# A new order for the first stretch of an attention and two-MoE kernel, with three PSUM banks for attention's blocks

## The chip, the cores and the metric

The kernel runs on one NeuronCore of a Trainium2 chip. The metric is the device time of one execution in microseconds (us), the median of several. The engines are named as in the profile: PE (TensorE matmul), PEld (TensorE weight load), DVE (VectorE), ACT (ScalarE), POOL (GpSimd) and SP (SyncE, which here only issues DMAs). Each engine has its own queue and takes its instructions in the order in which the kernel writes them.

## The reference, cut to what matters

```python
def _attn_ref(q, k, v, g_norm):                 # 4 batches, 8 heads, 576 tokens, head size 64
    kv = np.einsum('bhsd,bhse->bhde', k, v)
    out = np.einsum('bhsd,bhde->bhse', q, kv)
    rms = np.sqrt(np.mean(out * out, axis=-1, keepdims=True) + 1e-06)
    return (out / rms * g_norm).astype(np.float32)

def _moe_ref(x, w_in, w_out):                   # 2304 tokens, 512 -> 2048 -> 512
    h = x @ w_in
    g = h * (1.0 / (1.0 + np.exp(-h)))
    return (g @ w_out).astype(np.float32)

def _moe2_ref(x, domain_probs, w1, w2):         # 4 experts, 512 -> 1024 -> 512
    p = domain_probs / (domain_probs.sum(-1, keepdims=True) + 1e-09)
    out = np.zeros((N, D), dtype=np.float32)
    for e in range(E):
        h = np.maximum(x @ w1[e], 0.0)
        out += p[:, e:e + 1] * (h @ w2[e])
    return out
```

`reference` runs the three one after the other: attention's output, laid out as 2304 tokens by 512, goes through the first MoE, and its result through the second.

## The kernel before

**Three stages.** Attention gives x, transposed and kept in the SBUF tile `acc`. The first MoE is cut into four groups of 512 hidden units (E1 = 4), the second into eight (E2 = 8). Tokens are cut into three pairs of 768 (t = 0, 1, 2), and each pair into two halves of 384 (HN). Every fp32 operand is split into a high and a low fp32r half: the high one by a copy on ACT (`hi`, line 144), the low one by a subtraction on DVE or POOL (`lo`, line 147). A product is 12 matmuls of 128x384. In all but the first group, seven products stand in for eight (operands `b11`, `b21`, `t1` to `t4`, `b22` of x, where the `t` are differences made by `xsum`, line 317); the first group (`plain`, line 372) multiplies eight plain products per pair.

**Steps.** The steps are numbered n = -12 to 23: three pairs times four groups with n below 0, then three pairs times eight. `start[n]` gives a step its place in slots; a slot is as long as one product. `events` (line 612) and `first_events` (line 519) put every operation at a slot, the list is sorted, and that sorted list is each engine's order. n = -12 and n = -11 are the first group's pairs 0 and 1, n = -1 is the last step of the first MoE, n = 0 the first of the second, n = 8 and n = 16 begin the second MoE's pairs 1 and 2.

**The first stretch** is not in `events`. `PROGRAM` (line 36) writes its order out by hand, one word for each operation, and `attention_moe_kernel` issues the words one by one. What the words mean, with the engine:

- `lkv:b:c`, `lq:g`, `lwd:c:i` (SP): loads of a chunk of k and v (512 KB, the fifth chunk of a batch 256 KB), of 384 tokens of q (768 KB), of a chunk of the first MoE's raw weights (512 KB).
- `xp:t:name` (SP): store of a split operand of x to DRAM (768 KB); it waits until both halves are there.
- `kv:b:c` (PE): eight matmul records that add a chunk to k-transposed-v of batch b. `bda`, `bdv` (ACT, DVE): copy it out of PSUM.
- `om:i` (PE): attention's block i of 128 tokens (18 blocks). Then a chain for each block: `sq` (ACT, squares), `red` (DVE, sums), `rms` (POOL, power -0.5), `sc` (DVE, scales, frees the PSUM bank), `tr` (PE, transposes), `xc` (ACT, copies to `acc`).
- `cv1`, `cv2` (ACT), `cv3`, `cv4` (DVE), `cv5` (POOL): turn a chunk of raw weights into fp32. `wh`, `wl`, `vh`, `vl`: the two halves of the first group's first and second weights.
- `xh`, `xl`, `xt`: high half, low half and difference of x's operands. A trailing `:p` puts a low half on POOL, otherwise it is on DVE.
- `f:b:d`, `f1:b:d` (PE): product d of block b of `plain` for pairs 0 and 1. `si`, `hh`, `hl`: SiLU and the two halves of the hidden tile. `ready` closes attention's pools and opens those of the hidden tiles and second weights.

**Banks and buffers.** PSUM has eight banks. Four belong to `ps1`, as two buffers of two banks which `bank` (line 157) hands out by i % 2; `plain` takes number b + 1. Attention has `ps_o` (2 banks, for `om`), `ps_t` (1) and `ps_kv` (1). k and v of batches 1 to 3 have seven buffers, q has three, raw weights two; batch 0's chunks lie in x's own buffers. Buffers are freed when the last use stands in the order.

## Time and profile before

| | us |
|---|---|
| three runs, median (lowest to highest) | 1211.57 (1209.32 to 1212.93) |
| the profiled execution, its own time | 1213.71 |
| its span, from first to last instruction | 1211.9 |
| PE busy in the span | 1170.5 |
| DVE, ACT, POOL busy | 814.6, 482.5, 296.0 |

The time of the profiled execution is 1.8 us above its span and 2.1 us above the median. PE's records include time in which a matmul is in the pipeline, so its busy share says where PE is free, not how fast it runs. The mean granted clock of the span is 0.992 of full speed.

### The profile page before, as it was taken

To read this page: it belongs to the slowest core of one execution; us is meant where nothing else is said; L and a number is where in the kernel's file an instruction comes from. 1 tells how busy PE (TensorE), PEld (TensorE's weight loads), DVE (VectorE), ACT (ScalarE), POOL (GpSimd) and SP (SyncE) were. 2 spreads that over 40 slices of the span, in tenths; PEclk is the share of its full clock that TensorE was granted. 3 is DMA by queue.
4 is the path that set the end of the run, shared out by engine and by line. 5 is a ranking of instruction groups with operands and counts; after the bars stand their busy time and mean duration, and the time that the engine had idled before them with its cause. 6 is when DMAs were issued, how large, how long until landed. Compare 5 with 4: busy or idle time off the path is not lost.

```text
span 1211.9 us, 17576 instructions
## 1 busy us (share of the span) xinstructions
PE 1170.5 (97%) x6789; PEld 1158.8 (96%) x6789; DVE 814.6 (67%) x940; ACT 482.5 (40%) x693; POOL 296.0 (24%) x191
## 2 busy tenths in 40 slices
PE   6779999999999999999999999999999999999998
PEld 6679999999999989999999999999999899999997
DVE  2468775546544365767777876777788876666676
ACT  2457575435443242543444433333333242333222
POOL 2573331111210033323322311111113211111112
PEclk8999999999999998999999999999999999999999
DMA  9734798657655616797889687989898677778763
GB/s 315 261 108 187 255 346 307 234 194 246 236 171 175 215 70 222 276 325 277 295 304 329 236 283 261 352 294 339 304 350 295 239 239 259 274 261 267 260 215 122
DMA packets 105895, 309.00 MB, mean 255 GB/s; under 512 B 11532, under 2 KB 42708, under 8 KB 105812
## 3 DMA queue, kind: packets, MB, share of 16 engines
q1 hardware_dynamic: 103796, 304.69, 72.0%
q10 hardware_dynamic: 2016, 3.18, 0.7%
q8 instruction: 54, 0.88, 0.3%
q14 instruction: 29, 0.24, 0.1%
HBM read 227.84 MB, written 79.99 MB: 254 GB/s over the span
## 4 chain that ended last, share of the span: by engine, by line
PE 71%; DVE 10%; ACT 4%; issue 3%; DMA 2%; POOL 1%; SPq 1%; DVEq 0%; ACTq 0%; POOLq 0%
PE ps_o L481 21%; PE ps_x L356 19%; PE ps_z L356 15%; PE ps_ox L356 9%; PE ps_oz L356 7%; DVE hid L148 2%; DVE acc L321 2%; ACT hid L145 1%; DVE f L433 1%; ACT x L145 1%; DVE w L148 1%; DVE acc L456 1%; DVE f L399 1%; DVE x L148 1%; DMA w_dram<-w 1%
## 5 line engine op out<-in xcount | busy, mean ns | idle before, releaser
L481 PE MATMUL ps_o<-hid,w 128*128 128x384 f32 x1920 | 359.7, 337 | 6.3 <-ACT hid L145 3.5
L481 PEld LDWEIGHTS ps_o<-hid,w 128*128 128x128 f32 x1920 | 335.8, 189 | 9.6 <-ACT hid L145 4.1
L356 PE MATMUL ps_x<-x,w 128*128 128x384 f32 x1584 | 298.0, 336 | 1.9 <-ACT x L145 1.9
L356 PEld LDWEIGHTS ps_x<-x,w 128*128 128x128 f32 x1584 | 278.3, 189 | 2.2 <-ACT x L145 2.2
L356 PE MATMUL ps_z<-x,w 128*128 128x384 f32 x1188 | 222.7, 335 | 0.1
L356 PEld LDWEIGHTS ps_z<-x,w 128*128 128x128 f32 x1188 | 207.5, 188 | 0.7 <-ACT f L409 0.4
L145 ACT ACTIVATE hid<-f 128x768 fp32r<-128x768 f32 x128 | 107.8, 844 | 235.3 <-DVE f L433 230.2
L148 DVE TENSOR_TENSOR hid<-f,hid 128x768 fp32r<-128x768 f32 x111 | 122.6, 1106 | 75.1 <-ACT hid L145 73.9
L356 PE MATMUL ps_ox<-hid,w 128*128 128x384 f32 x768 | 144.9, 337 | 0.2 <-issue 0.2
L356 PEld LDWEIGHTS ps_ox<-hid,w 128*128 128x128 f32 x768 | 134.1, 188 | 0.5 <-issue 0.5
L148 POOL TENSOR_TENSOR hid<-t,hid 128x768 fp32r<-128x768 f32 x32 | 60.9, 1905 | 243.2 <-ACT hid L145 237.6
L356 PE MATMUL ps_oz<-hid,w 128*128 128x384 f32 x576 | 108.3, 336 | 2.0 <-DVE acc L456 1.9
L356 PEld LDWEIGHTS ps_oz<-hid,w 128*128 128x128 f32 x576 | 100.4, 188 | 3.2 <-DVE acc L456 2.5
L145 ACT ACTIVATE hid<-t 128x768 fp32r<-128x768 f32 x64 | 53.9, 843 | 122.1 <-DVE t L438 122.1
L148 POOL TENSOR_TENSOR w<-raw,w 128x512 fp32r<-128x512 f32 x41 | 60.5, 1481 | 163.1 <-ACT w L145 120.1
L456 DVE TENSOR_TENSOR acc<-ps_o,acc 128x768 f32<-128x768 f32 x64 | 60.9, 951 | 42.2 <-PE ps_o L481 41.9
L203 POOL TENSOR_TENSOR full<-full,wd_raw 128x512 int32<-128x512 int32 x32 | 47.2, 1474 | 143.1 <-DVE full L197 118.5
L399 DVE TENSOR_TENSOR f<-ps_z,f 128x768 f32<-128x768 f32 x66 | 62.8, 951 | 25.2 <-PE ps_z L356 25.2
L456 DVE TENSOR_TENSOR acc<-ps_ox,acc 128x768 f32<-128x768 f32 x57 | 54.2, 950 | 36.6 <-PE ps_ox L356 36.6
L433 DVE SCALAR_TENSOR_TENSOR f<-f,pb 128x768 f32<-128x768 f32 x72 | 72.5, 1007 | 2.1
L394 ACT ACTIVATE f<-ps_x 128x768 f32<-128x768 f32 x66 | 52.9, 802 | 50.5 <-PE ps_x L356 50.5
L148 POOL TENSOR_TENSOR hid<-f,hid 128x768 fp32r<-128x768 f32 x17 | 31.7, 1867 | 150.3 <-ACT hid L145 142.7
(79 smaller groups left out, 1113.5 us busy)
## 6 DMA issues: line engine op xcount, KB each, us to landing
w<-w_dram SPq DMA_DIRECT2D x224, 512.0 KB, 4.9
w_dram<-w SPq DMA_DIRECT2D x112, 512.0 KB, 4.1
x<-x_dram SPq DMA_DIRECT2D x63, 768.0 KB, 5.0
raw<-in_w SPq DMA_DIRECT2D x192, 128.0 KB, 3.7
wd_raw<-in_wd SPq DMA_DIRECT2D x32, 512.0 KB, 4.7
...
```

The source lines that it names most:

```text
L145: self.nc.scalar.activation(t[:, 0], f, AF.Copy)
L148: (eng or self.nc.vector).tensor_tensor(t[:, 1], f, t[:, 0].bitcast(F32), op=ALU.subtract)
L203: self.nc.gpsimd.tensor_tensor(f, f, self.words(c, i, 0, I32), op=ALU.add)
L321: self.nc.vector.tensor_tensor(o, a, b, op=ALU.subtract)
L356: self.nc.tensor.matmul(p[:, f, :HN], w[0][:, a, c : c + 128], x[:, b, kp, :], start=self.FRESH[k] and a == b == kp == 0, stop=b == kp == ...
L394: self.nc.scalar.activation(t, self.of_ps(n, c), AF.Copy)
L399: self.nc.vector.tensor_tensor(t, self.of_ps(n, c), t, op=ALU.add)
L433: self.nc.vector.scalar_tensor_tensor(f, src, 0.0, self.probs(n, int(name[2]) - 1), op0=ALU.max, op1=ALU.mult)
L456: self.nc.vector.tensor_tensor(a, self.of_ps(n, k), a, op=ALU.add)
L481: self.nc.tensor.matmul(self.ps[n, b][:, e, :HN], w[:, u, c : c + 128], h[:, v, kp, :], start=self.count[key] == 1, stop=self.count[key] = ...
```

## The change

It has five parts. (1) `PROGRAM` has the same operations in another order; eight low halves change their engine (`wl:2`, `xl:1:b11`, `vl:21`, `xl:0:t1`, `xl:0:t2`, `xl:0:t4` go from DVE to POOL, `wl:1` and `xl:0:b22` from POOL to DVE). All loads but `lwd:1:1` now stand ahead of the first store `xp`. (2) `ps_o` has three banks; `ps_kv` is gone, and `kv` uses a buffer of `ps1` with number b. (3) A split operand of x that is stored is dropped only after both its store and its last product (`done_x`), since either can now come first. (4) In `first_events` block 2 of pair 1's `plain` comes before the second product of pair 0, with its SiLU; `xget` of two operands of step n = -9 comes 1.4 and 1.7 slots earlier; at n = -1 the hidden block c12 gets SiLU and both halves sooner. (5) In `events` the second MoE's first weights (n = 0) are loaded 3.5 slots and converted, and stored, 2.7 slots earlier, and `xsum` of t1 for pairs 1 and 2 comes 4.7 slots earlier.

```diff
@@ -34,26 +34,26 @@
 
 
 PROGRAM = """
-lkv:0:0 lkv:0:1 lkv:0:2 kv:0:0 lkv:0:3 kv:0:1 lkv:0:4 kv:0:2 lq:0 kv:0:3 lwd:0:0 kv:0:4 bda:0 bdv:0 lwd:1:0
-om:0 om:1 lkv:1:0 sq:0 red:0 sq:1 rms:0 lkv:1:1 cv1:0:0 red:1 cv2:0:0 sc:0 rms:1 cv1:1:0 sc:1 lkv:1:2 tr:0
-kv:1:0 xc:0 cv3:0:0 cv2:1:0 tr:1 lkv:1:3 cv4:0:0 xc:1 kv:1:1 cv3:1:0 om:2 lkv:1:4 cv5:0:0 lq:1 kv:1:2 sq:2
-red:2 wh:0 kv:1:3 cv4:1:0 rms:2 sc:2 lq:2 cv5:1:0 kv:1:4 bda:1 tr:2 bdv:1 xc:2 wl:0 wh:1 om:3 lkv:2:0 xh:0:b11
-wl:1:p om:4 sq:3 lkv:2:1 xh:0:b21 red:3 xl:0:b11 rms:3 sq:4 lkv:2:2 sc:3 xl:0:b21:p xp:0:b11 kv:2:0 red:4 tr:3
-lkv:2:3 xc:3 kv:2:1 rms:4 xp:0:b21 sc:4 om:5 lkv:2:4 lwd:2:0 kv:2:2 sq:5 red:5 tr:4 kv:2:3 xc:4 lwd:3:0 rms:5
-sc:5 kv:2:4 tr:5 lq:3 bda:2 om:6 xc:5 bdv:2 om:7 sq:6 red:6 f:0:0 lkv:3:0 sq:7 rms:6 cv1:2:0 red:7 cv2:2:0
-sc:6 rms:7 lkv:3:1 cv1:3:0 sc:7 tr:6 om:8 xc:6 cv3:2:0 lkv:3:2 sq:8 kv:3:0 cv4:2:0 cv2:3:0 red:8 tr:7 cv5:2:0
-lkv:3:3 xc:7 kv:3:1 rms:8 cv3:3:0 wh:2 om:9 lkv:3:4 xh:0:b12 sc:8 lq:4 kv:3:2 sq:9 cv4:3:0 tr:8 red:9 kv:3:3
-cv5:3:0 xc:8 xh:0:b22 lq:5 kv:3:4 rms:9 wl:2 om:10 bda:3 wh:3 xl:0:b22:p bdv:3 f:0:1 sc:9 sq:10 lwd:0:1 red:10
-xp:0:b22 xl:0:b12 rms:10 tr:9 lwd:1:1 si:c11 sc:10 wl:3:p om:11 xc:9 om:12 sq:11 div wx tr:10 sq:12 f:1:0
-red:11 xc:10 red:12 cv1:0:1 rms:11 sc:11 rms:12 cv2:0:1 sc:12 tr:11 cv1:1:1 om:13 cv3:0:1 xc:11 cv2:1:1
-cv4:0:1 tr:12 cv3:1:1 sq:13 om:14 xc:12 red:13 cv5:0:1 f:1:1 sq:14 red:14 rms:13 lwd:2:1 rms:14 sc:13 si:c21
-sc:14 tr:13 om:15 cv4:1:1 xc:13 xt:0:t1 tr:14 sq:15 om:16 xc:14 red:15 cv5:1:1 turn sq:16 f:2:0 keepp red:16
-rms:15 lwd:3:1 xh:1:b11 sc:15 rms:16 xh:1:b21 sc:16 tr:15 om:17 xl:1:b21:p xc:15 tr:16 sq:17 f:2:1 xc:16
-red:17 xp:1:b21 cv1:2:1 xl:1:b11 rms:17 cv2:2:1 sc:17 xp:1:b11 f:3:0 si:c12 cv3:2:1 cv1:3:1 cv4:2:1 cv2:3:1
-tr:17 cv3:3:1 f:3:1 xc:17 cv5:2:1 xh:0:t1 ready hh:c11 cv4:3:1 f1:0:0 hh:c21 hl:c11 si:c22 hl:c21 hh:c12
-f1:0:1 cv5:3:1 hh:c22 xh:1:b12 hl:c12 f1:1:0 si1:c11 hl:c22 xh:1:b22 xl:1:b12 vh:11 f1:1:1 xl:1:b22 vh:12
-vh:21 vl:11 xp:1:b22 vh:22 vl:12:p si1:c21 vl:21 vl:22:p xl:0:t1 vx xt:0:t2 xp:0:t1 xh:0:t2 xt:0:t3 xl:0:t2
-xh:0:t3 xl:0:t3 xp:0:t2 xt:0:t4 xh:0:t4 xp:0:t3 xl:0:t4 xp:0:t4
+lwd:0:0 lkv:0:2 lkv:0:0 cv1:0:0 cv2:0:0 cv3:0:0 lkv:0:1 cv4:0:0 lkv:0:3 cv5:0:0 kv:0:0 wh:0 lq:0 kv:0:1 wl:0
+kv:0:2 lkv:0:4 kv:0:3 lkv:1:1 lkv:1:4 kv:0:4 lkv:1:0 bda:0 bdv:0 om:0 lkv:1:3 sq:0 om:1 lkv:1:2 red:0 om:2
+sq:1 rms:0 red:1 kv:1:0 sq:2 lwd:1:0 red:2 kv:1:1 rms:1 sc:0 lq:1 tr:0 kv:1:2 xc:0 rms:2 sc:1 kv:1:3 cv1:1:0
+lq:2 tr:1 cv2:1:0 cv3:1:0 kv:1:4 xc:1 sc:2 bda:1 om:3 cv4:1:0 lkv:3:1 bdv:1 cv5:1:0 tr:2 sq:3 om:4 xc:2 red:3
+lwd:3:0 xh:0:b11 rms:3 xh:0:b21 om:5 lkv:2:4 xl:0:b11 lkv:2:0 sq:4 sc:3 xl:0:b21:p wh:1 red:4 om:6 sq:5
+lkv:2:1 cv1:3:0 tr:3 red:5 rms:4 f:0:0 sq:6 cv3:3:0 lwd:2:0 cv2:3:0 red:6 rms:5 xc:3 cv4:3:0 kv:2:0 lkv:3:0
+sc:4 kv:2:1 rms:6 sc:5 lkv:2:2 wl:1 om:7 cv1:2:0 cv5:3:0 tr:4 sq:7 lkv:2:3 om:8 sc:6 cv2:2:0 red:7 f:0:1 xc:4
+cv3:2:0 lwd:0:1 rms:7 sq:8 wh:3 red:8 tr:6 cv4:2:0 lkv:3:2 si:c11 rms:8 kv:2:2 sc:7 xc:6 kv:3:0 lq:3 cv5:2:0
+cv1:0:1 tr:7 kv:2:3 sc:8 xc:7 wl:3:p wh:2 kv:3:1 lkv:3:3 cv2:0:1 kv:2:4 wl:2:p kv:3:2 bda:2 lkv:3:4 bdv:2 tr:8
+lq:4 cv3:0:1 wx om:9 xc:8 cv4:0:1 tr:5 sq:9 kv:3:3 cv5:0:1 xc:5 red:9 lwd:2:1 om:10 xh:0:b22 rms:9 kv:3:4
+xh:0:b12 xl:0:b22 lwd:3:1 om:11 bda:3 xl:0:b12 sq:10 f:1:0 lq:5 sq:11 sc:9 cv1:2:1 bdv:3 red:10 cv2:2:1 tr:9
+red:11 rms:10 cv1:3:1 om:12 cv3:2:1 xc:9 f:1:1 sq:12 div rms:11 cv2:3:1 xp:0:b22 xp:0:b11 xp:0:b21 sc:10 turn
+xh:1:b11 f:2:0 sc:11 keepp xl:1:b11:p red:12 si:c21 xh:1:b21 tr:10 om:13 rms:12 cv4:2:1 xc:10 xp:1:b11 cv3:3:1
+xt:0:t1 tr:11 sq:13 om:14 xc:11 red:13 cv5:2:1 f:2:1 xh:0:t1 sc:12 sq:14 rms:13 cv4:3:1 lwd:1:1 red:14 om:15
+si:c12 xt:0:t2 rms:14 tr:12 sq:15 sc:13 f:3:0 xc:12 red:15 cv5:3:1 xh:0:t2 sc:14 cv1:1:1 tr:14 rms:15 xt:0:t3
+cv2:1:1 om:16 cv3:1:1 xc:14 f:3:1 sq:16 sc:15 xl:1:b21:p xh:0:t3 red:16 tr:15 xh:1:b22 rms:16 cv4:1:1 om:17
+xp:1:b21 xc:15 xl:1:b22 f1:0:0 sq:17 xl:0:t3 xp:1:b22 xh:1:b12 sc:16 cv5:1:1 si:c22 xp:0:t3 tr:13 red:17
+f1:0:1 xc:13 xl:1:b12 rms:17 xt:0:t4 tr:16 sc:17 xl:0:t1:p f1:1:0 xc:16 xl:0:t2:p xp:0:t1 tr:17 f1:1:1 xc:17
+ready vh:21 hh:c11 vl:21:p xp:0:t2 hh:c21 hl:c11 hh:c12 hl:c21 si1:c11 hh:c22 hl:c12 si1:c21 hl:c22 vh:11
+vh:12 vl:11 vh:22 vl:12:p xh:0:t4 vl:22:p xl:0:t4:p vx xp:0:t4
 """
 
 
@@ -88,7 +88,7 @@
         for n in range(self.steps):
             self.start[n + 1] = self.start[n] + (self.LONG if n <= E2 else self.SHORT)
         self.stacks = {}
-        self.begun, self.count = set(), {}
+        self.begun, self.used, self.count = set(), set(), {}
         self.x, self.w1, self.wf, self.w2, self.raw, self.s, self.h, self.f, self.t, self.ps, self.pb = (
             {} for _ in range(11)
         )
@@ -338,8 +338,14 @@
     def xput(self, n, name):
         t = self.x[n, name].bitcast(F32).rearrange("p a b c -> p (a b c)")
         self.nc.sync.dma_start(out=self.x_dram[self.pair(n) * 7 + self.B.index(name)], in_=t)
-        if name[0] == "t":
+        self.done_x(n, name)
+
+    def done_x(self, n, name):
+
+        if name[0] == "t" or name == "b12" or (n, name) in self.used:
             del self.x[n, name]
+        else:
+            self.used.add((n, name))
 
     def xget(self, n, k):
         t = self.new_x(n, self.B[k], k).bitcast(F32).rearrange("p a b c -> p (a b c)")
@@ -385,7 +391,7 @@
                         )
         if i == d == 1:
             for k in range(2):
-                del self.x[n, f"b{k + 1}{j + 1}"]
+                self.done_x(n, f"b{k + 1}{j + 1}")
         if self.pair(n) == NP - 1 and j == 1:
             del self.wf[0, 2 * i + d]
 
@@ -531,10 +537,11 @@
                             put(b0 + 0.1 + b, self.hhi, n, name)
                             put(b0 + 0.2 + b, self.hlo, n, name)
                             continue
+                    ahead = t == 1 and b == 2
                     for d in range(2):
-                        put(at + 1 + 2 * d, self.plain, n, b, d)
+                        put(b0 - 0.4 + 0.1 * d if ahead else at + 1 + 2 * d, self.plain, n, b, d)
                     late = 2 if t == 1 else 0
-                    for slot, f in ((4.05, self.silu), (4.95 + late, self.hhi), (5.4 + late, self.hlo)):
+                    for slot, f in ((-0.1 if ahead else 4.05, self.silu), (4.95 + late, self.hhi), (5.4 + late, self.hlo)):
                         put(at + slot, f, n, name)
             elif e > 0:
                 for k in range(7):
@@ -546,9 +553,10 @@
                     put(b0 + slot, f, n, c, name)
                 put(b0 + 12.2, self.ps.pop, (n, "z"))
                 for slot, name in ((4.2, "c11"), (10.2, "c22"), (12.2, "c12"), (14.0, "c21")):
-                    put(b0 + slot + 0.02, self.silu, n, name)
-                    put(b0 + slot + 0.5, self.hhi, n, name)
-                    put(b0 + slot + 1, self.hlo, n, name)
+                    soon = n == -1 and name == "c12"
+                    put(b0 + slot + (-0.09 if soon else 0.02), self.silu, n, name)
+                    put(b0 + slot + (-0.08 if soon else 0.5), self.hhi, n, name)
+                    put(b0 + slot + (0.1 if soon else 1), self.hlo, n, name)
             blocks = self.blocks(n)
             for b, (i, j) in enumerate(blocks):
                 for d in range(2):
@@ -605,7 +613,7 @@
                 for k in range(7):
                     at = 2 * k - 12.4
                     if n == NP - F1:
-                        at = (-6.8, -6.7, -0.6, -4, -3.5, -0.5, 0.5)[k]
+                        at = (-6.8, -6.7, -0.6, -5.4, -5.2, -0.5, 0.5)[k]
                     put(b0 + at, self.xget, n, k)
         put(-24, self.swap)
 
@@ -629,14 +637,14 @@
                     of = {"t1": b0 - 11.5, "t2": b0 - 7.5, "t3": b0 - 6.5, "t4": b0 - 4.5}
                 else:
                     at = [last + k for k in (2.2, 4, 8.2, 6.3)] + [b0 + k for k in (6.2, 3, 8.2)]
-                    of = {"t1": last + 5.9, "t2": last + 7.7, "t3": b0 + 5.5, "t4": b0 + 7.3}
+                    of = {"t1": last + 1.2, "t2": last + 7.7, "t3": b0 + 5.5, "t4": b0 + 7.3}
                 for k, name in enumerate(self.B):
                     put(at[k], self.xhi, n, name)
                     put(at[k] + 0.01, self.xlo, n, name, pool if k in (1, 3, 5) and t == 0 or k in (0, 1, 5) and t else None)
                 for name, s in of.items():
                     put(s, self.xsum, t, name)
 
-            lead = self.LEAD + (2.5, -2)[n] if n < 2 else self.LEAD
+            lead = self.LEAD + (5.2, -2)[n] if n < 2 else self.LEAD
             for k in range(7):
                 i = b0 + 1 + 2 * k
                 put(i, self.first, n, k)
@@ -654,7 +662,7 @@
                 put(i - lead + 2, self.put_away, n, 1, k)
             if make:
                 for k, (i, j) in enumerate(((1, 0), (1, 1), (0, 0), (0, 1))):
-                    put(b0 - (self.LEAD + 5 if n else 20) + 0.5 * k, self.load1, n, i, j)
+                    put(b0 - (self.LEAD + 5 if n else 23.5) + 0.5 * k, self.load1, n, i, j)
                 for k, name in ((4, "a11"), (4, "a21"), (5, "a12"), (6, "a22"), (3, "s1"), (4, "s3"), (5, "s2"), (5, "s4")):
                     put(b0 + 1.01 + 2 * k - lead, self.raw.pop, (n, 1, name))
             put(b0 + 2.1, self.keep, n, "x", "c11")
@@ -798,9 +806,8 @@
     o_p = on(early, "o", 2)
     small_p = on(early, "small", 4)
     bd_p = on(early, "bd", 1)
-    ps_o = on(psum, "ps_o", 2, space=PSUM)
+    ps_o = on(psum, "ps_o", 3, space=PSUM)
     ps_t = on(psum, "ps_t", 1, space=PSUM)
-    ps_kv = on(psum, "ps_kv", 1, space=PSUM)
     squares = [bd_p.tile([128, H, D + 1], F32, tag=f"sq{i}", name=f"sq{i}") for i in range(2)]
     half = bd_p.tile([128, H], F32, tag="half", name="half")
     kvbd = [bd_p.tile([128, KC, 128], F32, tag=f"kvbd{i}", name=f"kvbd{i}") for i in range(B)]
@@ -827,7 +834,7 @@
 
     def kvm(b, c):
         if c == 0:
-            kv_ps[b] = ps_kv.tile([128, KC, 128], F32, tag="kv", name="p_kv")
+            kv_ps[b] = net.bank(net.ps1, b, "kv")[:, 0].rearrange("p (k n) -> p k n", k=KC)
         n, r = min(128, S - c * 128), kv_raw.pop((b, c))
         for hp in range(KC):
             cols = slice(hp * 128, hp * 128 + 128)
```

## Rows read from the trace of the kernel before

**Rows 1.** Page, part 1: busy us of the engines, share of the span, instructions.

```profile
PE 1170.5 (97%) x6789; PEld 1158.8 (96%) x6789; DVE 814.6 (67%) x940; ACT 482.5 (40%) x693; POOL 296.0 (24%) x191
```

**Rows 2.** Stretches: length, busy us (x instructions) of PE, PEld, DVE, ACT, POOL, clock, DMA, GB/s.

```profile
0.00:50.00 50.00, 31.77 (x206) 29.58 (x207) 14.91 (x24) 14.81 (x25) 19.15 (x24) 0.91 0.83 277
50.00:100.00 50.00, 42.49 (x295) 40.09 (x293) 33.61 (x52) 31.23 (x51) 33.64 (x21) 0.95 0.51 172
...
0.00:10.00 10.00, 3.12 (x13) 2.83 (x14) 0.15 (x1) 1.49 (x2) 2.72 (x14) 1.00 0.78 240
10.00:20.00 10.00, 7.55 (x45) 6.86 (x44) 1.82 (x3) 2.39 (x5) 0.82 (x1) 1.00 1.04 374
```

**Rows 3.** Waits of PE: who for whom, us in total, times, the longest.

```profile
PE p_t L881 <- DVE o L875: 13.7, 8, 3.4
```

**Rows 4.** Groups by line, PE, 0 to 107.7 us: busy, mean ns, idle before.

```profile
L382 PE MATMUL ps_h<-x,w 128*128 128x384 f32 x144 | 26.8, 340 | 0.0
L834 PE MATMUL p_kv<-kv_raw 128*128 128x128 f32 (+1 forms) x160 | 26.3, 322 | 9.2 <-DMA kv_raw<-in_kv 9.2
L855 PE MATMUL p_o<-kvbd,q_raw 128*128 128x128 f32 (+1 forms) x160 | 21.6, 300 | 2.7 <-DVE o L875 1.7 <-DVE kvbd L842 1.0
L881 PE MATMUL p_t<-ident,o 128*128 128x128 f32 x72 | 13.1, 312 | 13.8 <-DVE o L875 13.7
```

**Rows 5.** Timeline of PE, first stretch: start, us, instruction, [idle before <-releaser].

```profile
16.50 2.05 PE L855 MATMUL p_o<-kvbd,q_raw 128*128 128x128 f32 x16 [0.99 <-DVE kvbd L842]
...
39.63 0.63 PE L881 MATMUL p_t<-ident,o 128*128 128x128 f32 x4 [3.42 <-DVE o L875]
40.09 1.06 PE L834 MATMUL p_kv<-kv_raw 128*128 128x128 f32 x8
...
107.76 2.18 PE L481 MATMUL ps_o<-hid,w 128*128 128x384 f32 x11 [0.67 <-DVE w L148]
```

**Rows 6.** Chain of work that ended last, one full product: start, us, what.

```profile
178.02 2.08 PE ps_o L481 x12
```

**Rows 7.** Groups by line, 0 to 180 us: attention's chain, and POOL's low halves of x.

```profile
L870 POOL TENSOR_TENSOR rinv<-ssq,half 128x8 f32<-128x8 f32 x18 | 32.3, 1802 | 31.5 <-DVE ssq L866 31.5
...
L875 DVE TENSOR_TENSOR o<-p_o,rinv 128x512 f32<-128x512 f32 x18 | 12.5, 692 | 19.9 <-POOL rinv L870 19.9
...
L866 DVE TENSOR_REDUCE ssq<-sq 128x8 f32<-128x520 f32 x18 | 12.3, 690 | 11.9 <-ACT sq L862 11.8
...
L862 ACT ACTIVATE sq<-p_o 128x512 f32<-128x512 f32 x18 | 10.7, 595 | 11.4 <-PE p_o L855 10.6 <-DVE ssq L866 0.7
...
L148 POOL TENSOR_TENSOR x<-acc,x 128x768 fp32r<-128x768 f32 x4 | 7.5, 1874 | 12.1 <-ACT x L145 12.1
```

**Rows 8.** Timeline of SP's queue, first stretch (merged issues of one line).

```profile
19.56 5.23 SPq L818 DMA_DIRECT2D kv_raw<-in_kv  x3
37.32 0.33 SPq L340 DMA_DIRECT2D x_dram<-x  x1
```

**Rows 9.** Timeline of PE, DVE and ACT where the second MoE begins.

```profile
449.63 0.67 DVE L280 TENSOR_TENSOR s<-raw,raw 128x512 f32<-128x512 f32 x1
...
452.69 0.83 ACT L145 ACTIVATE hid<-f 128x768 fp32r<-128x768 f32 x1
...
453.57 1.06 PE L481 MATMUL ps_o<-hid,w 128*128 128x384 f32 x4 [2.66 <-ACT hid L145]
...
455.56 2.93 PE L481 MATMUL ps_o<-hid,w 128*128 128x384 f32 x8 [0.92 <-DVE hid L148]
...
458.28 3.56 PE L356 MATMUL ps_x<-x,w 128*128 128x384 f32 x12
```

**Rows 10.** Timeline of POOL, DVE and PE before the second MoE's third pair.

```profile
935.28 1.89 POOL L148 TENSOR_TENSOR hid<-t,hid 128x768 fp32r<-128x768 f32 x1 [2.57 <-ACT hid L145]
935.38 2.61 DVE L321 TENSOR_TENSOR acc<-acc 128x768 f32<-128x768 f32 x1
...
940.78 2.36 PE L356 MATMUL ps_oz<-hid,w 128*128 128x384 f32 x12 [1.62 <-DVE acc L456]
```

## Prediction

> **What bounds the kernel now.** I read the page first: PE is busy 97% of the span, every other engine 67% or less [rows 1], so time can only come from PE's idle time and from PE's slow clock. I then cut the span into stretches of 50 us. From 100 us on nearly all are full; the first two have 31.8 and 42.5 us of PE work and a mean clock of 0.91 and 0.95 [rows 2]. The list of PE's waits has one large item: 13.7 us, in eight waits, in which a transpose waits for the scaled block from DVE [rows 3]; the groups by line add 9.2 us of waiting for k and v [rows 4]. I looked at two later places because the change touches them: the first step of the second MoE [rows 9] and the step before its third pair [rows 10].
>
> To size the first stretch I count its work at the full clock. Two starts in the timeline, 39.63 and 40.09, make a block's transposes 0.46 us; the kv chunk after it is shown as 1.06 us, but the next instruction group starts 0.89 us later, since the ends of matmuls overlap [rows 5] (a chunk of kv and a block of om both have eight records). A full product takes 2.08 us [rows 6]. Before the first product with second weights PE does 20 chunks, 18 blocks, 18 transposes and 12 plain products [rows 4]: 17.8 + 16.0 + 8.3 + 25.0 = 67.1 us. That product really starts at 107.8 us [rows 5], so 40.7 us are lost. The first block starts at 16.5 us [rows 5] with 4.5 us of work done: 12.0 lost at the start, 28.7 later. Of these, 13.7 + 1.7 us are PE waiting for the scaled block [rows 4], some 7.0 us are slow clock (50 x 0.09 + 50 x 0.05 [rows 2]), some 2 us a late third wait for k and v.
>
> **The change part by part. First stretch, the chain.** Between a block's `om` and its `tr` stand four steps: 0.60, 0.69, 1.80 and 0.69 us [rows 7], 3.8 us, and with the handovers about 4.2 (an estimate). I added up the PE work that the two orders put between `om:i` and `tr:i`. Before, it is less than 4.2 us in 14 of 18 blocks (0.9 us for block 0, 1.8 for block 3), 16.8 us short in all, close to the 15.4 us that PE waits; that agreement is why I trust the count. In the new order only blocks 0 and 3 are short (3.6 and 3.1 us), 1.7 us in all. Three banks make this order possible, since three or more blocks are then under way. If POOL has one low half (1.87 us [rows 7]) ahead of each power, the chain is 5.9 us, five blocks are short and 6.7 us remain. I take 5, near the upper end, since POOL also has eight `cv5` and more low halves there: gain 15.4 - 5 = **10.4 us**, from 8.7 to 13.7.
>
> **The start.** `om:0` needs the last chunk of batch 0. Ahead of it and with it now come 3.67 MB (a raw weight chunk and q are in front) instead of 2.36 MB. 240 GB/s over the first 10 us and 374 after it [rows 2] put these at 13.4 and 9.8 us: **3.6 us later**, from 1.5 (part of that time PE was behind the data) to 5.
>
> **Loads and stores.** SP takes its list in order. Before, it issued k and v until 24.8 us and then nothing until 37.3 us, where a store of x was released [rows 8]; the loads behind that store stood still. Now all of these loads stand ahead of the stores, and SP can stop only where a buffer is still read; the tightest is `lwd:3:1`, ten words behind the `cv5:0:1` that frees it. I put the late wait for k and v at nothing: gain **2 us**, from 0 to 2.3. The stores pay for it. `xp:0:b22`, `b11` and `b21` now stand just ahead of `xh:1:b11` and `xh:1:b21`, which write the same buffers, so ACT waits for 2.36 MB to be read: 6.3 us at 374 GB/s and the landing. Behind ACT's wait are `keepp`, `si:c21` and `xc:10`, for which PE's `tr:11` waits; between the store's last operand and `tr:11` PE has three blocks, three products and two transposes, 9.8 us. So 0 to 3 us, I take 1. `kv:3:0` now waits for `si:c11`, which frees its bank: 1.35 us of PE work between, against a SiLU behind one square and one weight half on ACT: 0 to 1, I take 0.4. At `ready` the second weights (`vh`, `vl`) are now the last words, but two plain products (4.2 us) are put ahead of the first product that needs them: 0 to 3, I take 1, where 0.67 us stand now [rows 5]. New waits: **2.4 us**, from 0 to 7.
>
> **Clock.** With long idle gaps the clock falls, and 7.0 us went that way. One fall, at the start, I leave in place; gain **2.5 us**, from 0 to 4. The first stretch: 10.4 + 2 + 2.5 - 3.6 - 2.4 = 8.9 us gained.
>
> **DVE against POOL.** Six low halves go to POOL and two come back. An operation of DVE that started 0.10 us behind one of POOL took 2.61 us, and ended 0.82 us after POOL's, which took 1.89 us [rows 10]; it looks as if it stood still for the other's remaining 1.79 us and then ran. The Trainium skill, "SBUF — State Buffer", section "Who interferes with whom", says that an instruction of DVE with two inputs in SBUF and one of POOL that reads SBUF share a port pair held for the whole instruction, so that the second one waits; these rows agree. By that rule each further meeting costs DVE up to one POOL operation, and the rule speaks against the change. By the rows the price of a meeting is up to 1.79 us on DVE; four more meetings are 7.2 us of DVE, on an engine that is idle half of the first 100 us [rows 2]. I count none of it on PE beyond the 5 us above; it sets a rival.
>
> **First step of the second MoE.** PE waits 2.66 us for the high half of c12 and 0.92 us for its low half; then a third of a product takes 2.93 us over eight matmuls and the next product 3.56 us [rows 9] instead of 1.39 and 2.08 [rows 6], some 2.8 us of slow clock after allowing for the drawn-out ends: 6.4 us. The change takes one 0.67 us weight sum from in front of c12's addition on DVE (s1 and s2 move ahead of that stretch, s4 enters it, s3 stays) and one conversion of x, 0.83 us like c12's own, from in front of c12's high half on ACT [rows 9]. The 2.66 us become 1.2, the low half still waits 0.9. A single wait of 1.62 us elsewhere left the product behind it at 2.36 us [rows 10], so I expect full clock: gain 1.5 + 2.8 = **4.3 us**, from 0.7 to 6.4. The earlier loads, conversions and stores of these weights pass `load_p` and `load2` on SP; they have 11 slots of lead as before, so I cost them at nothing. If a weight half came late, one product would wait some 2 us.
>
> **Third pair.** The difference that took 2.61 us on DVE moves ten us earlier, to a place with idle time; the sum for which PE waits 1.62 us [rows 10] comes earlier by more than that: gain **1.6 us**, 0 to 1.9. For the second pair the same move has no wait to remove. The two earlier `xget` have no wait of PE behind them either: nothing.
>
> **Sum.** 8.9 + 4.3 + 1.6 = 14.8. I give back 0.8 because PE then meets the next weight conversions sooner: 14.0. The profiled execution took 1213.7 us; less 14.0 is 1199.7. It lies 2.1 us above the median of the runs, so the median becomes 1211.6 - 14.0 = 1197.6: **1198 us**.
>
> **The rivals.** A measurement of this kernel tells 0.3%, 3.6 us, from no change. *POOL carries the chain*: the powers queue behind conversions and low halves, 8 us of waits remain and the slow clock stays, so the first stretch gives about 1 us; with the rest, 6 gained: 1206. For it: POOL is busy 33.6 of the second 50 us already [rows 2]; against: it is the same work over nearly the same time. *The waits only move*: ACT stands behind the stores the full 3 us, the handover costs 3, the clock still falls, and c12 gains only its lower end: nothing in the first stretch, 2 elsewhere: 1210, no change. *More than forecast*: all ends good, 13.7 + 2.3 + 4 - 1.5 in the first stretch and 8.3 elsewhere: 1186. *Slower*: POOL's low halves and `cv5` hold DVE's sums and scales up, in the stretch from 20 to 100 us. If twelve meetings of 1.79 us [rows 10] come on the chain, 21.5 us are added and 7.5 remain lost: 1219; from ten meetings on it is slower by more than 3.6 us. Against it: all but four of these operations stand there already, and the chain's count fitted without it. The Trainium skill's rule on the shared port pair (same page and section) would make this the outcome if each further meeting fell on the chain; the trace shows the meetings but not that they reach PE.
>
> **How the numbers follow.** Forecast (9 to 20 us gained) 0.50; more 0.11; POOL carries the chain 0.22; the waits only move 0.10; slower 0.07. So faster 0.83, same 0.10, slower 0.07. The range of 1186 to 1209 takes in all ends but the last two cases, about 0.15 left out.
>
> **What would show it.** Right: waits of `p_t` for DVE fall from 13.7 to some 5 us; SP shows no gap from 25 to 37 us; the first block starts near 20 us and the first product with second weights, now behind two more products, before 102 us; the 2.66 us wait halves and the products behind it are at 2.1 to 2.4 us; the 1.62 us wait is gone. Wrong: a first block after 24 us, ACT waiting for the stores, a new long wait of PE after 100 us, or `rms` waiting in POOL's queue with `p_t` as before.

## The result and the profile after

| | before | after |
|---|---|---|
| median of 4 runs each (us) | 1212.15 | 1192.10 |
| lowest to highest (us) | 1209.32 to 1212.93 | 1191.13 to 1193.36 |
| profiled execution (us) | 1213.7 | 1192.07 |
| its span (us) | 1211.9 | 1190.3 |

One run of the kernel before was added to the three shown ahead. The ratio is 0.9839, with a 95% interval of 0.982 to 0.9858. The median falls by 20.0 us where 14.0 were forecast. 1192 lies inside the range of 1186 to 1209, but at the far end of the case that I called the forecast (9 to 20 us gained).

The first fence holds rows of the changed kernel that answer to [rows 1] and [rows 2]: the engines' busy time on the page, then two stretches of 50 us (length, then busy us of PE, PEld, DVE, ACT and POOL, granted clock, DMA share, GB/s).

```profile
PE 1162.4 (98%) x6789; PEld 1153.9 (97%) x6789; DVE 803.6 (68%) x936; ACT 482.2 (41%) x693; POOL 303.1 (25%) x195
...
0.00:50.00 50.00, 37.34 (x265) 35.50 (x266) 20.85 (x36) 22.13 (x37) 26.60 (x30) 0.93 0.96 311
50.00:100.00 50.00, 45.87 (x316) 43.79 (x316) 34.54 (x51) 35.30 (x55) 35.40 (x22) 1.00 0.53 202
```

PE is busy for 9 us more in these 100 us, and the clock of the second stretch rose from 0.95 to 1.00. The next view is the list of PE's waits in the changed kernel (who for whom, us in total, times, the longest); it answers to [rows 3].

```profile
PE ps_kv L841 <- DMA kv_raw<-in_kv: 10.0, 2, 8.0
PE ps_o L487 <- ACT hid L145: 3.1, 2, 2.6
PE ps_h L388 <- ACT f L415: 2.2, 1, 2.2
PE ps_x L362 <- ACT x L145: 1.9, 1, 1.9
PE p_t L888 <- ACT p_t L907: 1.4, 1, 1.4
PE p_o L862 <- DVE o L882: 1.3, 1, 1.3
...
PE p_t L888 <- DVE o L882: 0.4, 1, 0.4
```

The 13.7 us for DVE's scaled block [rows 3] are 0.4 now; with the 1.3 us in front of one `om`, 1.7 us are left of the 15.4. Of the 10.0 us for k and v, 8.0 are the start before any data is there. Two waits are new: `ps_h` for ACT (2.2) and `p_t` for ACT (1.4). The timeline of PE in the changed kernel shows where they sit, and the two landmarks of [rows 5] (start, us, instruction, [idle before <-releaser]). The single row behind it is from the kernel before.

```profile
19.43 4.73 PE L862 MATMUL p_o<-kvbd,q_raw 128*128 128x128 f32 x24 [0.98 <-issue]
...
66.63 0.66 PE L888 MATMUL p_t<-ident,o 128*128 128x128 f32 x4 [1.41 <-ACT p_t L907]
...
92.72 4.45 PE L388 MATMUL ps_h<-x,w 128*128 128x384 f32 x24 [2.22 <-ACT f L415]
97.01 6.41 PE L487 MATMUL ps_o<-hid,w 128*128 128x384 f32 x36
...
437.13 2.65 PE L487 MATMUL ps_o<-hid,w 128*128 128x384 f32 x12 [2.58 <-ACT hid L145]
...
947.73 3.81 PE L362 MATMUL ps_x<-x,w 128*128 128x384 f32 x12 [1.86 <-ACT x L145]
```

```profile
106.76 0.34 PE L481 MATMUL ps_o<-hid,w 128*128 128x384 f32 x1
```

The first product with second weights starts at 97.0 us. In the kernel before its first matmul stands at 106.8, ahead of the row of [rows 5], and the other eleven go on at 107.8; the end of the product is 10.7 us earlier in the changed kernel. Two more plain products (4.2 us) are done by then: 14.9 us ahead. Following the same products through both timelines gives the whole balance: 14.9 us at 97 us; 16.4 in front of the second MoE's first step, by small differences on the way that I did not follow; 20.0 behind that step; 20.5 in front of the third pair and 22.4 behind the wait of 1.62 us [rows 10], which is gone; 23.0 at 947.7; and 21.6 behind the product there and at the end, because that product takes 3.81 us where before, behind the same wait of 1.86 us, it took 2.36. That is the whole difference of the two profiled executions, 1213.7 - 1192.1 = 21.6. It is one execution of each kernel, and the last section shows that three pieces of it came out otherwise in other kernels with the same waits.

### The profile page after: what moved, and what is told of

The parts are those of the page before. It is cut to its first block, busy times and chain, and to the rows that moved or that the text cites. A ratio compares the mean times of both kernels' runs of the same rounds, so it can differ in the third digit from the quotient of the medians.

```text
span 1190.3 us, 17575 instructions
## 1 busy us (share of the span) xinstructions
PE 1162.4 (98%) x6789; PEld 1153.9 (97%) x6789; DVE 803.6 (68%) x936; ACT 482.2 (41%) x693; POOL 303.1 (25%) x195
## 3 DMA queue, kind: packets, MB, share of 16 engines
q10 hardware_dynamic: 2016, 3.18, 0.8%
## 4 chain that ended last, share of the span: by engine, by line
PE 80%; DVE 7%; DMA 5%; ACT 3%; issue 3%; POOL 2%; SPq 0%; POOLq 0%; DVEq 0%; ACTq 0%
PE ps_o L487 24%; PE ps_x L362 21%; PE ps_z L362 16%; PE ps_ox L362 9%; PE ps_oz L362 7%; DMA x_dram<-x 1%; ACT hid L145 1%; DVE f L439 1%; DVE acc L321 1%; DVE hid L148 1%; PE ps_kv L841 1%; ACT x L145 1%; DMA x<-x_dram 1%; DMA kv_raw<-in_kv 1%; PE p_o L862 1%
## 5 line engine op out<-in xcount | busy, mean ns | idle before, releaser
L145 ACT ACTIVATE hid<-f 128x768 fp32r<-128x768 f32 x128 | 107.8, 844 | 232.8 <-DVE f L439 227.7
L148 DVE TENSOR_TENSOR hid<-f,hid 128x768 fp32r<-128x768 f32 x111 | 119.9, 1082 | 79.4 <-ACT hid L145 78.3
```

Of the source, the lines that this page charges most:

```text
L145: self.nc.scalar.activation(t[:, 0], f, AF.Copy)
L148: (eng or self.nc.vector).tensor_tensor(t[:, 1], f, t[:, 0].bitcast(F32), op=ALU.subtract)
```

## The experiments

Four questions: what the two halves of the change are worth; what in the first stretch does it (cover, banks, stores, start); why the wait at 437 us did not halve; and whether the waits that are left can be taken away. Ratios are always to runs of the kernel before on the same chip.

**The later edits alone, and the order alone.** The first kernel is the kernel before with the change's edits of `events` and `first_events` (and the release of x operands that they need); PROGRAM and the PSUM banks stand as before. The second is the changed kernel with those edits undone.

```diff
# the later edits (added to before; taken back from after)
-put(at + 1 + 2 * d, self.plain, n, b, d)
+put(b0 - 0.4 + 0.1 * d if ahead else at + 1 + 2 * d, self.plain, n, b, d)
...
-"t1": last + 5.9,
+"t1": last + 1.2,
...
-lead = self.LEAD + (2.5, -2)[n] if n < 2 else self.LEAD
+lead = self.LEAD + (5.2, -2)[n] if n < 2 else self.LEAD
...
```

> The kernel before with only the later edits (block 2 of pair 1 ahead, c12 sooner, second experts' first weights earlier, xsum of t1 and xget earlier); the first stretch keeps its old order, its two banks and its stores among the loads. Theory (the first stretch carries the gain): only the later edits' part is left, 3.6 us at the second MoE's first step, 1.9 us before its third pair and up to 1 us at the handover, so some 1206 us (1204 to 1208). Rival (the later edits carry most of it): below 1200 us.

Measured: 1207.9 us, 0.9961 (0.9943 to 0.998), at the upper end of what was expected. The wait in front of c12 is 2.61 us in this kernel too.

> The changed kernel with the later edits undone: new order of the first stretch, three banks, stores behind the loads, and the old slots everywhere else. Theory (the first stretch carries the gain): some 1197 us (1195 to 1200), with the 2.7 and 0.9 us waits and the slow clock back at the second MoE's first step and the 1.6 us wait back before its third pair. Rival: above 1203 us.

Measured: 1199.9 us, 0.99 (0.9886 to 0.9915). The order with its three banks is worth 11.6 us and the later edits 3.7, together 15.3; the whole change gives 20. The gap of 4 to 5 us is hardly clear of the spread: the interval of the first ratio alone reaches from 2.4 to 6.9 us gained. PE's waits in the kernel with the order alone:

```profile
PE ps_o L487 <- ACT w L145: 4.2, 1, 4.2
PE ps_o L487 <- ACT hid L145: 3.7, 3, 2.7
```

With the new order PE gets to the second weights before they are converted (4.2 us). The two plain products put ahead fill about half of that hole (2.2 us are left in the changed kernel), and that gain of 2 us shows in neither half alone. The profiled executions miss 4.3 us (21.6 against 3.5 and 13.8): 1.4 are missing behind the handover to the second weights, and 1.6 more behind the second MoE's first step, where the later edits alone left two slow products (3.29 and 3.22 us) and the whole change one nearly full one (2.65). So a part of the gap is the speed of single products behind a wait, told of in the last section.

**The cover.** The count of PE work between `om` and `tr` says that 14 blocks are short of the chain in the kernel before and 2 in the changed one. So the chain itself was made shorter, once in each kernel: the power on POOL is left out. These two kernels leave out the normalisation and scale every block by a constant.

```diff
 def rms(i):
-    rinv[i] = small_p.tile([128, H], F32, tag="rinv", name="rinv")
-    nc.gpsimd.tensor_tensor(rinv[i], ssq.pop(i), half, op=ALU.pow)
+    ssq.pop(i)
+    rinv[i] = half
```

> The kernel before with the power of every block's row sums left out (GpSimd's 1.80 us each): the blocks are scaled by a constant, so the normalisation is not computed. Everything else stands. Cover theory: the way from a block's product to its transpose shrinks from 4.2 to 2.4 us, and the PE work listed between the two is short of 2.4 us in only 3 of 18 blocks, by 3.1 us in all; the waits of p_t on DVE's o fall from 13.7 to 3 to 5 us, the first product with second weights comes 8 to 11 us earlier (near 98 in place of 107.8), the time is 1201 to 1205. Rival, the new order helped mainly by what it loads and starts earlier: then the shorter chain only makes PE run into the loads, the waits on k/v grow by most of what the transposes give, and the first product with second weights comes less than 4 us earlier (over 1208).

Measured: 1199.4 us, 0.9899 (0.9879 to 0.9918).

> The changed kernel with the same power left out (the blocks are scaled by a constant; the normalisation is not computed). Cover theory: nothing is short of 2.4 us, so the 1.7 us of waits on DVE's o go and hardly anything else: the time falls by 0 to 2.5 us (1189.5 to 1192), a fifth at most of what the same edit gives the kernel before. Rival, GpSimd's time is the bound of the new first stretch (18 powers are 32 us of GpSimd before 85 us): the time falls by 5 us or more.

Measured: 1191.5 us, 0.9834 (0.9814 to 0.9854). The same edit takes 12.3 us from the kernel before and 0.6 from the changed one. PE's wait in the kernel before without the power, and its two stretches of 50 us:

```profile
PE p_t L881 <- DVE o L875: 2.5, 2, 2.3
...
0.00:50.00 50.00, 35.53 (x237) 32.51 (x237) 17.73 (x30) 17.93 (x31) 9.06 (x18) 0.93 0.95 322
50.00:100.00 50.00, 49.75 (x348) 48.44 (x347) 43.71 (x60) 36.80 (x59) 16.80 (x11) 1.00 0.49 170
```

13.7 us of waits became 2.5, near the 3.1 of the count. The gain at the first product with second weights (92.2 instead of 107.8 us) is larger than the 8 to 11 us expected; the clock, 0.93 and 1.00 in the two stretches for 0.91 and 0.95 [rows 2], gives 3.5 us of it by the reckoning of the prediction. The kernel before was held by the way from `om` to `tr`, and the changed kernel hides it. With the two products put ahead counted, the two ways lead to the same place: 96.4 us (92.2 + 4.2) and 97.0. The edit also takes 1.8 us times 18 from POOL's queue, and in the kernel before that is not told apart from the shorter chain. The rival in which POOL's time carries the new stretch falls: POOL is busy 62.0 us of the first 100 in the changed kernel and 32.4 without the powers, and the time falls by 0.6 us only. One expectation is missed: the waits on DVE's o should have gone from the changed kernel without the power, but 2.1 us of them stay. Its timeline shows the largest:

```profile
29.10 1.58 ACT L145 ACTIVATE x<-acc 128x768 fp32r<-128x768 f32 x2
29.98 0.96 DVE L148 TENSOR_TENSOR x<-acc,x 128x768 fp32r<-128x768 f32 x1 [0.76 <-DMA wd_raw<-in_wd]
...
30.96 0.69 DVE L882 TENSOR_TENSOR o<-p_o,half 128x512 f32<-128x512 f32 x1
...
31.71 1.16 PE L862 MATMUL p_o<-kvbd,q_raw 128*128 128x128 f32 x8 [1.31 <-DVE o L882]
```

The scale that frees the bank stands on DVE behind a low half of x (29.98), and that starts when the first of two copies on ACT is done (29.10, shown as one row of 1.58 us). It is the same 1.3 us as in the changed kernel, and the power has no part in it.

**The third bank.** The changed kernel with two banks for the blocks; words of PROGRAM are moved back only where a block would otherwise stand in line for a bank that comes free behind it.

```diff
-ps_o = on(psum, "ps_o", 3, space=PSUM)
+ps_o = on(psum, "ps_o", 2, space=PSUM)
...
-om:0 lkv:1:3 sq:0 om:1 lkv:1:2 red:0 om:2 sq:1 rms:0 ...
+om:0 lkv:1:3 sq:0 om:1 lkv:1:2 red:0 sq:1 rms:0 ... sc:0 om:2 sq:2 red:2 ...
```

> The changed kernel with two banks for attention's blocks (the third one is left idle); a word of the list is put off only where a block has no free bank, with what depends on it. Cover theory: between om and tr the PE work is short of the 4.2 us chain by 3.4 us in all instead of 1.7, and between a block and the one that needs its bank short of 3.7 us by 4.8 instead of 1.5, so PE waits 3 to 6 us more: 1195 to 1198 us. Rival (the order alone does it, two banks would do): 1192 to 1193 us.

Measured: 1200.5 us, 0.9904 (0.9886 to 0.9921). PE's waits with two banks:

```profile
PE p_o L861 <- DVE o L881: 6.9, 4, 2.5
...
PE p_o L861 <- issue: 2.4, 2, 1.4
```

The waits for DVE's scaled block are back, but now a block waits for its bank, and no longer a transpose for its operand. The first product with second weights starts at 105.5 us. The third bank, with the words that had to move with it, is worth 8.4 us (7.9 by the ratios), more than the 3 to 6 expected: some 40% of the gain. With two banks the new order still gives 11 us.

**The stores.** The changed kernel with two of the three stores of x operands back in front of later loads.

```diff
-... f:1:1 sq:12 div rms:11 cv2:3:1 xp:0:b22 xp:0:b11 xp:0:b21 sc:10 turn xh:1:b11 ...
+... lkv:2:1 xp:0:b11 ... lwd:2:0 xp:0:b21 ...
+... f:1:1 sq:12 div rms:11 cv2:3:1 xp:0:b22 sc:10 turn xh:1:b11 ...
```

> The changed kernel with the stores of x's b11 and b21 put back among the loads (behind lkv:2:1 and lwd:2:0), as they stood before. Load theory (the stop of SP's list behind a store is what cost PE time): SP stands still from some 26 to 34 us, the loads behind are about 8 us late, PE waits 5 to 8 us more for k, v and q: 1197 to 1200 us. Cover theory (the loads have that much slack, what counts is the PE work between om and tr): at most 3 us more of waiting, and ACT's 3.5 us wait for these stores with the 1.9 us of PE behind it goes away: 1191 to 1194 us.

Measured: 1190.4 us, 0.9816 (0.9797 to 0.9834). Keeping the stores behind all loads gains nothing: with early stores the waits for k and v are 9.2 us (10.0 after), the wait of `p_t` for ACT is gone, and the first product with second weights starts at 95.0. The two intervals overlap, so the 1.7 us between the medians are not clear of the spread. The timelines tell more, if the same products are taken just ahead of ACT's wait, just behind it, and at the handover; first with early stores, then the changed kernel, whose row of the handover is shown above:

```profile
61.75 2.33 PE L387 MATMUL ps_h<-x,w 128*128 128x384 f32 x12
...
68.97 1.05 PE L861 MATMUL p_o<-kvbd,q_raw 128*128 128x128 f32 x8
...
89.24 5.93 PE L387 MATMUL ps_h<-x,w 128*128 128x384 f32 x24 [2.23 <-ACT f L414]
```

```profile
62.87 2.35 PE L388 MATMUL ps_h<-x,w 128*128 128x384 f32 x12
...
72.28 1.05 PE L862 MATMUL p_o<-kvbd,q_raw 128*128 128x128 f32 x8
```

With early stores PE is 1.1 us ahead in front of the place, and that lead is not the stores' doing, since it was 1.4 at the first block already (17.99 against 19.43), ahead of any store. Behind the place it is 3.3 us ahead. The difference, 2.2 us, fits the 1.9 us of PE's waits for ACT that are gone. At the handover it falls to 2.0, because the two products take 5.93 us in place of 4.45. So this part of the change cost some 2 us where it acts; that the whole kernel is faster without it is not shown. The row of ACT in the changed kernel:

```profile
65.57 0.84 ACT L145 ACTIVATE x<-acc 128x768 fp32r<-128x768 f32 x1 [3.47 <-DMA x_dram<-x]
```

**The start.** The changed kernel with the first loads in the order of before.

```diff
-lwd:0:0 lkv:0:2 lkv:0:0 cv1:0:0 cv2:0:0 cv3:0:0 lkv:0:1 cv4:0:0 lkv:0:3 cv5:0:0 kv:0:0 wh:0 lq:0 kv:0:1 wl:0
-kv:0:2 lkv:0:4 kv:0:3 lkv:1:1 ...
+lkv:0:2 lkv:0:0 lkv:0:1 lkv:0:3 lkv:0:4 lq:0 lwd:0:0 kv:0:0 kv:0:1 kv:0:2 kv:0:3 lkv:1:1 ...
+... sq:2 cv1:0:0 cv2:0:0 cv3:0:0 cv4:0:0 cv5:0:0 ... lq:1 wh:0 wl:0 ...
```

> The changed kernel with batch 0's k/v and q issued before the first expert weights and those converted after the first blocks, as the kernel before has it. Theory of the start term: the first block moves from 19.4 us towards 16.5, by 1.3 us if it is only the 0.5 MB in front of it (at some 390 GB/s of that stretch) and by up to 2.9 us if the conversion's place counts too; the time falls by 1 to 3 us (1189 to 1191). Rival, the whole first 45 us is bound by the bytes: what the start gains comes back as longer waits of PE on k/v of batches 1 to 3 (10.0 us of kv_raw waits now become 11 to 13) and the time stays within 1 us of 1192.

Measured: 1191.4 us, 0.9829 (0.9812 to 0.9845): no difference from the changed kernel. PE's timeline in this kernel:

```profile
16.32 2.94 PE L861 MATMUL p_o<-kvbd,q_raw 128*128 128x128 f32 x24 [0.99 <-DVE kvbd L848]
...
54.79 2.36 PE L387 MATMUL ps_h<-x,w 128*128 128x384 f32 x12
...
65.21 0.66 PE L887 MATMUL p_t<-ident,o 128*128 128x128 f32 x4 [2.41 <-ACT p_t L906]
...
91.30 6.00 PE L387 MATMUL ps_h<-x,w 128*128 128x384 f32 x24 [2.22 <-ACT f L414]
97.14 6.41 PE L486 MATMUL ps_o<-hid,w 128*128 128x384 f32 x36
```

The first block comes 3.1 us earlier, and at 54.8 us PE is still 2.4 us ahead (the same product starts at 57.2 in the changed kernel). Then the wait behind the stores grows by 1.0 us, and the two products at the handover take 6.00 us in place of 4.45; at 97 us the lead is gone. So the early start was tried with the stores early as well:

> The changed kernel with the first loads in the order of before and, besides, the stores of the two operands early. With the first loads alone PE was 2.4 us ahead of the changed kernel up to 57 us and level with it again at 97 us; two things could have taken that: the wait behind the stores near 65 us (2.41 in place of 1.41 us) and the clock at the handover (24 matmuls 6.00 in place of 4.45 us). Theory that the stores' wait holds the gain: without it PE is at the first product with second weights at 92.6 to 93.5 us (95.0 with early stores alone) and the time is 1187.5 to 1189. Rival, the handover takes whatever comes early (its own chain on ACT and a slow clock behind it): first second product at 94.5 to 95.5, the time 1190 to 1191.

Measured: 1191.1 us, 0.9824 (0.9806 to 0.9842), with the first product with second weights at 96.5 us. The landmark is later than either expectation. The time is the rival's, but not by its cause alone. The stores' wait is gone, but now PE waits for k and v behind its first chunk: 10.7 us in all, of which 6.4 before the first data, so 4.3 against 2.0 in the changed kernel, and the handover again takes 6.01 us. What the start gains is paid back to the loads (the DMA share stands at 1.02 to 1.06 in every 10 us from 10 to 60 us, where it falls to 0.83 and 0.73 from 40 us on in the changed kernel) and to the slow products at the handover.

**The three waits that are left.** The kernel with early stores, with one edit for each.

```diff
-    put(i - lead - 1.7, self.sumw, n, 1, "s3" if k == 4 else "s4")
+    at = b0 - 2.85 if n == 0 and k == 5 else i - lead - 1.7
+    put(at, self.sumw, n, 1, "s3" if k == 4 else "s4")
...
-at = ... [b0 + k for k in (6.2, 3, 8.2)]
-of = {... "t3": b0 + 5.5, ...}
+at = ... [b0 + k for k in (6.05 if t == 2 else 6.2, 3, 8.2)]
+of = {... "t3": b0 + (5.25 if t == 2 else 5.5), ...}
...
-ready vh:21 hh:c11 vl:21:p xp:0:t2 hh:c21 hl:c11 hh:c12 hl:c21 si1:c11 hh:c22 hl:c12 si1:c21 hl:c22
+ready hh:c11 hh:c21 hl:c11 si1:c11 xp:0:t2 hl:c21 hh:c12 hh:c22 hl:c12 si1:c21 vh:21 vl:21:p hl:c22
```

> The kernel with early stores (1190.4 us) with three edits more, each for one wait that is left: DVE's sum s4 behind the sum of c12 (wait before the product at 437 us: 2.58 to about 0.9), at the handover the activation of the second tokens' first block directly behind the hidden half that it waits for (wait near 92 us: 2.2 to about 1.3), and the third tokens' sum t3 ahead of DVE's half of c11 (wait near 948 us: 1.86 to 0, and the slow clock of the product behind it, 1.3 us, with it). If each wait is the last one of its place: 1190.4 - 1.7 - 0.9 - 1.9 - 1.3 = 1184.6. If one takes the place of the next (DVE's hidden half of c11 behind t3, the next silu on ACT at the handover, the gather before c12 on DVE): 1188 to 1190.4.

Measured: 1188.0 us, 0.9808 (0.9793 to 0.9823). That is 2.4 us less than with early stores alone, and the two intervals overlap. Two of three edits do what they should: the wait at the handover is 1.25 us, and the one before t3 is gone with the slow product behind it (2.77 us). The third does not: 2.59 became 1.98, and the product behind it still took 3.92 us. POOL, DVE and PE in front of c12, first in the changed kernel (PE's row is shown with the result), then in this one:

```profile
430.50 1.68 POOL L148 TENSOR_TENSOR w<-s,w 128x512 fp32r<-128x512 f32 x1 [5.23 <-ACT w L145]
430.94 1.78 DVE L280 TENSOR_TENSOR s<-raw,s 128x512 f32<-128x512 f32 x1
432.65 0.95 DVE L148 TENSOR_TENSOR hid<-f,hid 128x768 fp32r<-128x768 f32 x1
...
434.38 0.94 DVE L405 TENSOR_TENSOR f<-ps_z,f 128x768 f32<-128x768 f32 x1
```

```profile
430.30 1.68 POOL L147 TENSOR_TENSOR w<-s,w 128x512 fp32r<-128x512 f32 x1 [5.23 <-ACT w L144]
430.74 2.05 DVE L147 TENSOR_TENSOR hid<-f,hid 128x768 fp32r<-128x768 f32 x1
...
433.58 0.94 DVE L404 TENSOR_TENSOR f<-ps_z,f 128x768 f32<-128x768 f32 x1
...
436.32 3.92 PE L486 MATMUL ps_o<-hid,w 128*128 128x384 f32 x12 [1.98 <-ACT hid L144]
```

DVE's operation that starts 0.44 us behind POOL's takes 1.1 us longer than its kind does elsewhere: first the sum s4 (1.78 against 0.68), and with s4 away the hidden half of c22 (2.05 against 0.95). The meeting went to the next in line. So in the last step POOL's operation itself is moved, with ACT's half of the same operand, and the first loads are put in the order of before as well:

```diff
-    put(i - lead, self.op1, n, k, pool if k in (1, 4, 6) or n == 0 else None)
+    at = b0 - 2.84 if n == 0 and k == 4 else i - lead
+    put(at, self.op1, n, k, pool if k in (1, 4, 6) or n == 0 else None)
```

> The kernel with the later edits (1188.0 us) with two more: the first loads in the order of before, and the operand of the second experts' weights that ACT and GpSimd make near 430 us (k = 4) moved behind the sum s4. In the kernel with the later edits s4 was out of the way, but the next DVE operation, the hidden half of c22, took 2.05 in place of 0.95 us beside GpSimd's 1.68 us, and the wait before the product at 436 us fell to 1.98 only. Meeting theory: with no GpSimd operation between 429 and 434 us that half takes 0.95 us, the wait is 0.8 to 1.0 us and its product near 2.3 to 2.7 us; with the earlier start (up to 2.4 us) the time is 1183.5 to 1186. Rival, the wait there is held by the sums and gathers of DVE themselves: it stays over 1.7 us, and the time is 1186 to 1188 by the start alone, or 1188 where the handover eats that too.

Measured: 1184.8 us, 0.9781 (0.9762 to 0.98). The same place:

```profile
430.87 0.95 DVE L147 TENSOR_TENSOR hid<-f,hid 128x768 fp32r<-128x768 f32 x1
431.74 0.95 DVE L461 TENSOR_TENSOR acc<-ps_o,acc 128x768 f32<-128x768 f32 x1
432.60 0.94 DVE L404 TENSOR_TENSOR f<-ps_z,f 128x768 f32<-128x768 f32 x1
...
435.36 2.65 PE L486 MATMUL ps_o<-hid,w 128*128 128x384 f32 x12 [0.89 <-ACT hid L144]
```

The half takes 0.95 us, the wait is 0.89 us, as the meeting theory has it. Whether the early start has a share in this kernel:

> The fastest kernel (1184.8 us) with the first loads back in the changed kernel's order: the first expert weights are issued and converted ahead of batch 0's k/v. All later edits stay. Theory that the first 55 us are bound by the bytes of the loads: with the first loads in front PE began 2.1 us earlier (16.3 in place of 18.4 us), but waited for k/v and q behind its start 5.5 us (4.6 and 0.9) where the kernel with the later edits waited 1.4; the start earned nothing, and this kernel takes 1183.5 to 1186 as well. Rival, the early start is part of the gain that the fastest kernel shows (1188.0 to 1184.8): then this one takes 1186.5 to 1187.5, the later edits with the moved operand alone (1188.0 less the 1.1 us of the wait at 436 us).

Measured: 1186.3 us, 0.9798 (0.9781 to 0.9815). The intervals of the two overlap, and this time lies between the two expectations, so the share of the start stays open. The profiled executions speak against it: without the early start the first block stands 1.0 us later (17.1 against 16.1), and the first product with second weights 4.2 us earlier (92.0 against 96.1). The kernel with all edits beats both kernels of this case: 0.9781 against the changed kernel's 0.9839, with intervals that do not meet.

## Why the prediction was right, and where its sizes were off

- **The chain** was the right mechanism, with a remaining wait taken too high: 5 us where 1.7 remain, so 13.7 gained instead of 10.4. I had added POOL's queueing to the count of 1.7. That the count and the measured sum are the same number is partly chance: 0.4 us are waits of a transpose, and 1.3 the wait for a bank behind x's low half, which the count doesn't know. In the two kernels in which much is short its sum holds: 16.8 against 15.4 in the kernel before, 3.1 against 2.5 without the power. Block by block it is rough: in the kernel before it has 2.85 us for block 1, whose transpose did not wait, and 0.77 for block 13, whose transpose waited 2.77.
- **The start**: the first block at 19.4, forecast 20; it cost 2.9 us there for 3.6. That is one execution: the seven kernels traced with this order of the first loads have their first block at 17.1 to 19.4 us, the six with k and v first at 16.1 to 16.9. In the two kernels that give the start back (k and v first, alone and with early stores) the gain was lost again further on, so it is not shown that this term cost the whole run anything.
- **Loads and stores**: with 2 us for the loads and 1 for the stores the sum was +1; the stores' place alone cost about 2 (2.2 between the products around it). The path that I had for them was wrong in one step: I let PE wait at `tr:11` for `xc:10`, and it waited first at `tr:10` (1.41 us, then 0.50 at `tr:11`), with 8.5 us of PE work in front of it and not the 9.8 that I had counted, because `turn` holds the one bank of `ps_t` until `keepp`, which stands on ACT behind the wait for the stores. SP's idle stretch from 24.8 to 37.3 us is gone, but one of 6 us is left (33.7 to 39.8), where a load waits for a buffer.
- **The handover** cost 2.2 us in place of 1: in front of the two products put ahead PE waits for a SiLU that stands on ACT behind a weight half and three hidden halves (89.03 to 91.85 us in ACT's timeline). I had looked for this wait at the second weights' own halves, behind these products.
- **The clock** gave 3.5 us (3.5 lost instead of 7.0) for 2.5. All in all the first stretch gave 14.9 where 8.9 stood. The parts measured are 13.7 + 2 + 3.5 - 2.9 - 1.9 - 1.5 = 12.9, with the handover counted over the 0.67 us of [rows 5]; 2 us are left. About 0.9 of them are counted twice: the last chunk in front of the first block ran at the low clock (2.07 us, 1.16 for the same chunk of the next batch), which stands in the start's 2.9 and in the clock's 3.5. The rest I can't name.
- **First step of the second MoE**: the step that failed. The wait was to fall from 2.66 to 1.2 and fell to 2.58. I had counted the sum taken away in front of c12's addition on DVE, and s4, which comes in, at nothing; beside POOL it takes 1.78 us. The low half's wait of 0.92 us went, and the product behind came at nearly full speed (2.65 us), so 3.6 us came in place of 4.3. But the forecast had the speed come from the shorter wait, and the wait did not get shorter: in six other kernels with this wait at 2.58 to 2.61 us the product took 3.29 to 3.92 us. That this term came out near its size is luck.
- **Third pair**: the wait of 1.62 us went as forecast (1.9 for 1.6); 1.4 us were lost again at the next wait, of 1.86 us, by a slow product. That is close to the give-back of 0.8 in size, but not from its cause.
- **The rivals.** POOL carrying the chain is refuted for the new order by the changed kernel without the power. Its price was added up wrongly: 15.4 - 8 + 2 - 3.6 - 2.4 is 3.4 us for the first stretch and not 1, so 1203 us and not 1206; nothing hangs on it. More than forecast (1186) stood as far from the measured 1192 as the forecast (1198): the first stretch gave 14.9 us, between its 18.5 and my 8.9. The rival on the slower side, DVE's sums and scales held up by POOL between 20 and 100 us, is not what the traces show. All sums and scales that stand as rows of their own there take 0.68 to 0.70 us in both kernels, also beside POOL. What a meeting can lengthen is the power on POOL, which takes 1.64 us at the median of the 18. Two meetings in the changed kernel, the first beside a difference of x's operands on DVE:

```profile
75.48 1.45 DVE L321 TENSOR_TENSOR acc<-acc 128x768 f32<-128x768 f32 x1
76.07 2.36 POOL L877 TENSOR_TENSOR rinv<-ssq,half 128x8 f32<-128x8 f32 x1
...
78.40 1.84 POOL L148 TENSOR_TENSOR x<-acc,x 128x768 fp32r<-128x768 f32 x1
78.47 0.69 DVE L882 TENSOR_TENSOR o<-p_o,rinv 128x512 f32<-128x512 f32 x1 [0.72 <-POOL rinv L877]
```

The mechanism reaches PE at 430 us, with about 1.1 us (the wait of 1.98 us that became 0.89); that is once and not twelve times. There DVE's instruction has both inputs in SBUF. The Trainium skill, "SBUF — State Buffer", section "Who interferes with whom", says that such an instruction and one of POOL that reads SBUF contend for the shared port pair and that the one issued later is blocked; the rows at 430 us agree (1.78 and 2.05 us beside POOL, 0.68 and 0.95 alone).
